# Sliding-window attention beside a long convolution on one core: three spectral products instead of four, folded filter blocks, and a common tile layout

## The chip, the cores and the metric

The kernel runs on one core of a Trainium2 chip. The metric is the device time of one execution in microseconds; "before" is the median of three runs. A profile shows one execution with a span from its first to its last instruction.

The engines are named as in the profile: PE (TensorE, matmuls; PEld is its loading of weights), DVE (VectorE), ACT (ScalarE), POOL (GpSimd), SP (SyncE, which here only issues DMAs). SPq, ACTq and POOLq are the queues from which DMAs are issued. Each engine works through its own queue in order and waits on semaphores of the others.

## The reference

Two independent computations over 2048 positions and 576 channels, joined along the channels:

```python
# a: attention, 32 heads of 18, each position sees itself and 7 earlier ones, two apart
q, k, v = split(x @ wqkv)                       # 2048x576 times 576x1728
logits[s, w] = q[s] . k[s - 2 w] * 18 ** -0.5   # w = 0..7, masked before position 0
o = sum_w softmax(logits)[s, w] * v[s - 2 w]
a = o @ wo
# b: short convolution, gate, long causal convolution per channel, gate
k_shift[s] = sum_t k[s - t] * shift_k[:, t]     # 4 taps
kv = k_shift * v
y = causal_convolution(kv, ssm_k, length 2048)  # written with an FFT of 4096
b = q * (y + kv * ssm_D)
out = concatenate([a, b], axis=-1)
```

## The kernel before

**Stages.** Everything lies in one instruction stream per engine, written out by Python code. In order of time: a head (constants, loading and turning x, tables of sines); the taps of the short convolution on DVE while PE projects q and k; the attention (logits, softmax, weighing of v) on DVE while PE projects v and makes spectra; the spectral products on DVE while PE sums them, turns them back and multiplies by wo; and a short tail.

**The long convolution.** The sequence is cut into four blocks of 512 (`NBL`, `BL`), and so is the filter. Each block gets a spectrum of length 1024 by matmuls with tables of sines and cosines. `filter_spectrum(m)` (L520) makes eight units per filter block: a frequency group `gi` of 128 by a cosine or sine part `cs`; each unit is four steps `c` of 128 positions, each of two matmuls in `mm3` (L515 and L516, 384 and 192 columns), and one eviction by ACT to `Ks` (L530). `turn_filter` then adds the neighbouring block's parts with accumulating DMAs on POOL's queue (L542). `x_spectrum(i)` (L579) does the same for a block of kv, with eight units of eight half-height matmuls (L586) evicted to `xw` (L589). The input block is folded about its middle first by `mirror` (L490).

The output block j is the sum over i of spectrum x[i] times filter[j - i]. `products(j, t, i)` (L856) makes all four products of the two real parts for one third t of the channels, 4 x 768 = 3072 columns, in one DVE instruction (L860); there are 30, over four buffers. `sums` (L867) adds them on PE with signed identity matrices, 16 matmuls for each (L880), and ACT evicts to `Yall` (L893). `inverse` (L900) transforms back, turns back by `flip` matrices and gates with q.

**Attention.** `logits` (L615) multiplies q by four shifted k's on DVE (4096 columns, L624) into two buffers, and PE sums over each head by the 0/1 matrices `E` (L633). `softmax` (L642) runs on DVE apart from the exponent on ACT (L658). `spread` (L694) copies the weights of one head group to all its channels by four DMAs on SP's queue (L701), for six chunks (two halves of positions by three channel groups). `weigh` (L713) multiplies them by v on DVE (L723, 18 instructions) and sums on PE (L739, L753). `output` (L776) multiplies by wo.

**What sets the order.** DVE's sequence is fixed by the program. PE's is woven: projections, spectra, mirrors, inverse and wo steps are units in the list `units`, and `until()` (L282) inserts the next few, as many as the next number in `PLACES` says, ahead of the PE work of the current DVE step. `need(label)` inserts all up to a label. PSUM offers two double banks under each of the tags A and B, so a unit also waits until ACT has evicted the one two before it under its tag.

**Places of the change.** v's weights are loaded by `load_w` into a corner of `Ks` and copied into head order by `reorder` (five ACT copies, L561) among the first filter units. Tables come from `table_k(0..3)` and `table_x(0..1)` (two tensor_scalars at L373 and one at L374 on DVE, one sine at L375 on ACT for each). The D term is added through the matrix `ones0` and the row `Drow`. Spread weights lie in the tile `X0`, in `qk` and in `pv`.

## Time and profile before

| What | Value |
|---|---|
| runs | 224.41, 224.32, 224.28 us; median 224.32 |
| profiled execution | 225.0 us, of which the span is 223.0 |
| granted PE clock | 1.00 |
| ACT busy | 154.4 us |
| taps on DVE | 16.8 to 61.0 us |
| logits, softmax and weighing on DVE | 61.2 to 160.4 us |
| spectral products on DVE | 160.4 to 215 us |
| last instructions of DVE | 218.66 us |
| `attn` spreads on SP's queue | first issue at 99.23, last issued by 142.9 us |
| filter transposes on SP's queue | issued 40.4 to 48.7 and 50.5 to 59.4 us, 5.0 to 10.5 us to landing |

The page lists for each group of instructions the line, engine and operation, the tiles written and read, the shapes, the count, the busy time in us with the mean of one in ns, and then how long the engine was idle just before them and what ended that. In the timeline the columns are start, duration, engine, line, operation, and in brackets the idle time before. In the list of waits they are the waiter, whom it waited for, the total in us, how often, and the longest.

### The profile page before, as it was taken

To read this page: it belongs to the slowest core of one execution; us is meant where nothing else is said; L and a number is where in the kernel's file an instruction comes from. 1 tells how busy PE (TensorE), PEld (TensorE's weight loads), DVE (VectorE), ACT (ScalarE), POOL (GpSimd) and SP (SyncE) were. 2 spreads that over 40 slices of the span, in tenths; PEclk is the share of its full clock that TensorE was granted. 3 is DMA by queue.
4 is the path that set the end of the run, shared out by engine and by line. 5 is a ranking of instruction groups with operands and counts; after the bars stand their busy time and mean duration, and the time that the engine had idled before them with its cause. 6 is when DMAs were issued, how large, how long until landed. Compare 5 with 4: busy or idle time off the path is not lost.

```text
span 223.0 us, 5309 instructions
## 1 busy us (share of the span) xinstructions
PE 213.1 (96%) x2271; PEld 118.2 (53%) x2271; DVE 208.1 (93%) x156; ACT 154.4 (69%) x213; POOL 31.9 (14%) x68
## 2 busy tenths in 40 slices
PE   7999999999999999999999999999999999999891
PEld 2543444444566556753444445665656667666560
DVE  7789999999988999999899999999999899999992
ACT  5858766888596987756667768885678887655630
POOL 8860000000000040403410000015000000330000
PEclk9999999999999999999999999999999999999999
DMA  5999999999900047659999469917211103662016
GB/s 187 274 229 219 188 241 203 221 207 235 216 0 0 3 83 131 117 95 169 198 190 235 124 114 203 225 32 234 88 56 53 57 3 107 199 208 75 3 53 159
DMA packets 30985, 31.41 MB, mean 141 GB/s; under 512 B 16849, under 2 KB 26705, under 8 KB 30962
## 3 DMA queue, kind: packets, MB, share of 16 engines
q1 hardware_dynamic: 25714, 21.93, 44.6%
q0 software_dynamic: 2624, 6.64, 14.6%
q10 hardware_dynamic: 2624, 2.51, 3.3%
q8 instruction: 17, 0.28, 0.5%
q14 instruction: 6, 0.05, 0.1%
HBM read 13.11 MB, written 4.72 MB: 80 GB/s over the span
## 4 chain that ended last, share of the span: by engine, by line
PE 76%; DVE 9%; ACT 5%; issue 4%; DMA 3%; SPq 1%; DVEq 0%; ACTq 0%
PE ps_proj L310 15%; PE ps_fk L515 10%; PE ps_wo L792 7%; PE ps_fx L586 6%; DVE qk L860 6%; PE ps_z L880 5%; PE ps_log L633 5%; PE ps_fk L516 5%; PE ps_acc L739 4%; PE ps_inv L912 4%; PE ps_proj L427 3%; PE ps_proj L315 3%; DMA X<-attn 3%; PE ps_proj L322 3%; PE ps_idle L138 2%
## 5 line engine op out<-in xcount | busy, mean ns | idle before, releaser
L860 DVE TENSOR_TENSOR qk<-xw,Ks 128x3072 bf16<-128x3072 bf16 x30 | 50.5, 1750 | 1.2 <-PE ps_z L880 1.0
L624 DVE TENSOR_TENSOR prod<-qk 128x4096 bf16<-128x4096 bf16 (+1 forms) x20 | 40.6, 2074 | 3.4 <-PE ps_log L633 3.3
L310 PE MATMUL ps_proj<-xw 128*128 128x512 bf16 x160 | 38.4, 380 | 0.0
L515 PE MATMUL ps_fk<-kTok,TK 128*128 128x384 bf16 x128 | 32.8, 327 | 0.6 <-ACT Ks L530 0.5
L516 PE MATMUL ps_fk<-kTok,TK 128*128 128x192 bf16 x128 | 31.4, 246 | 0.0
L530 ACT ACTIVATE Ks<-ps_fk 128x576 bf16<-128x576 f32 x32 | 20.4, 653 | 9.9 <-PE ps_fk L516 9.7
L310 PEld LDWEIGHTS <-xw 128*128 128x128 bf16 x160 | 14.3, 98 | 18.9 <-issue 4.9
L893 ACT ACTIVATE Yall<-ps_z 128x768 bf16<-128x768 f32 x23 | 17.4, 808 | 6.1 <-PE ps_z L880 5.9
L346 ACT ACTIVATE qk<-ps_proj 128x1024 bf16<-128x1024 f32 x14 | 14.4, 1027 | 7.1 <-PE ps_proj L310 3.4
L589 ACT ACTIVATE xw<-ps_fx 128x576 bf16<-128x576 f32 x32 | 18.6, 660 | 0.2
L515 PEld LDWEIGHTS <-TK 128*128 128x128 bf16 x128 | 12.5, 98 | 11.8 <-issue 4.2
L792 PE MATMUL ps_wo<-qk,pv 128*128 128x288 bf16 x128 | 17.9, 287 | 0.0
L586 PE MATMUL ps_fx<-ab,TX 64*128 64x288 bf16 x256 | 17.7, 283 | 0.0
L487 DVE TENSOR_TENSOR ab<-ab,tB 128x2304 bf16<-128x2304 bf16 x12 | 16.3, 1358 | 0.4
L880 PE MATMUL ps_z<-qk,ident 64*64 64x384 bf16 x288 | 16.4, 325 | 0.3 <-ACT pv L743 0.3
L484 DVE TENSOR_TENSOR tB<-kj,skb 128x2304 bf16<-128x2304 bf16 x12 | 16.3, 1356 | 0.3
L912 PE MATMUL ps_inv<-Yall,TI 128*128 128x288 bf16 (+1 forms) x112 | 15.5, 292 | 0.7 <-ACT Yall L893 0.6
L739 PE MATMUL ps_acc<-P,ident 64*64 64x512 bf16 x192 | 15.3, 379 | 0.0
L346 ACT ACTIVATE v<-ps_proj 128x1024 bf16<-128x1024 f32 x9 | 9.2, 1022 | 8.8 <-PE ps_proj L322 4.6
L586 PEld LDWEIGHTS <-TX 64*128 64x128 bf16 x256 | 11.7, 94 | 6.5 <-issue 3.6
L799 ACT ACTIVATE qk<-ps_wo 128x576 bf16<-128x576 f32 x16 | 10.4, 651 | 6.1 <-PE ps_wo L792 3.0
L792 PEld LDWEIGHTS <-pv 128*128 128x128 bf16 x128 | 11.5, 98 | 6.0 <-issue 3.2
(146 smaller groups left out, 352.8 us busy)
## 6 DMA issues: line engine op xcount, KB each, us to landing
kj<-in_B_k_dram SPq DMA_DIRECT2D x7, 504.0 KB, 8.1
Ks<-Ks POOLq DMA_DIRECT2D x6, 576.0 KB, 7.7
qk<-attn SPq DMA_DIRECT2D x12, 256.0 KB, 5.8
vt<-in_B_v_dram SPq DMA_DIRECT2D x8, 288.0 KB, 8.6
out_dram<-qk ACTq DMA_DIRECT2D x8, 288.0 KB, 2.9
X<-attn SPq DMA_DIRECT2D x8, 256.0 KB, 5.1
Ks<-in_A_x_dram SPq DMA_DIRECT2D x2, 576.0 KB, 5.2
xw<-in_A_wqkv_dram SPq DMA_DIRECT2D x2, 576.0 KB, 7.4
```

Source lines behind the costliest of these rows:

```text
L310: nc.tensor.matmul(ps[:, jp, :], wq(kb, comp, 128 * ct, 128), xT(kb, 1024 * jj + 512 * jp, 512), start=(kb == 0 and not first), stop=(kb = ...
L346: nc.scalar.activation(view(t, o + pad + 1024 * jj, [[512, 2], [1, 512]]), ps[:], ACT.Copy)
L515: nc.tensor.matmul(o[:, 0:2], w, rhs[:, 0:2], start=start, stop=stop)
L516: nc.tensor.matmul(o[:, 2], w, rhs[:, 2], start=start, stop=stop)
L530: nc.scalar.activation(view(Ks, (3 - m) * SPB + 4 * D * cs + 96 * gi, [[768, 3], [384, 2], [1, 96]]), acc3(ps), ACT.Copy, scale=(CSG, SSG) ...
L586: nc.tensor.matmul(ps[:, pm, 0:HD], TX[64 * pm:64 * pm + 64, c, 128 * gi:128 * gi + 128], kv[64 * pm:64 * pm + 64, c, HD * h:HD * h + HD], ...
L624: r = dve(1024 * nj, lambda: nc.vector.tensor_tensor(view(prod, 0, [[256 * nj, 4], [256, nj], [1, 256]]), view(t, o + 256 * hh, [[0, 4], [ ...
L739: nc.tensor.matmul(acc[64 * o:64 * o + 64, h, :], ident[64 * h:64 * h + 64, 64 * h:64 * h + 64], view(P, 256 * u, [[2048, 2], [1, 256]])[6 ...
L792: nc.tensor.matmul(ps[:, r, 0:HD], oT(hh, j + 2 * r, t)[:, o:o + 128], wo[:, t // 2, t % 2, HD * h:HD * h + HD], start=(t == 0 and h == 0) ...
L860: r = dve(3072, lambda: nc.vector.tensor_tensor(pr, view(xw, i * SPB + 4 * TH * t, [[4 * D, 2], [0, 2], [1, 4 * TH]]), view(Ks, (3 - j + i ...
L880: nc.tensor.matmul(view(acc[r], 512 * h, [[192, 2], [96, 2], [1, 96]])[o:o + 64], w[64 * h:64 * h + 64, 64 * h:64 * h + 64], pr[64 * h:64 ...
L912: nc.tensor.matmul(ps[:, c, 0:n], TI[:, sl, pm, 128 * c:128 * c + 128], Yall[:, j % 2, pm, sl, c0:c0 + n], start=(pm == 0 and sl == 0), st ...
```

## The change

- **Products.** The spectra are held as sum and difference of their parts ("turned basis"), and each block of `xw` and of `Ks` has three parts: two from the evictions, and a third, their sum, that DVE adds when a block is first used (six additions of 768 and six of 2304 columns). A product is then 3 x 768 = 2304 columns; three buffers instead of four. PE's sums use identities of 1 and 2 with signs; their number stays at 480.
- **Filter blocks.** `fold_filter` folds a block about its middle: per block 8 or 12 matmuls (`ps_rev`), two ACT evictions of 576 columns scaled by 0.5, a scaling of one row on POOL, and an accumulating DMA of 2 x 576 columns for the partner. A spectrum unit then has two steps instead of four (for two of eight units one more, with the constant `two`). `table_k` runs twice instead of four times. D is added to the filter's first row by a DMA; `first_rows` exchanges rows by six DMAs of one row on SP's queue.
- **v's weights** are loaded once and read by PE with a step of nine elements, 64 columns at a time (`wa`), instead of being copied in order by ACT.
- **Softmax.** The reciprocal of the sums on DVE becomes Ln and Exp(-x) on ACT.
- **Layout.** `xw`, `Ks`, `TB`, `av`, `v` and `qk` are cut into equal parts of 2304 columns (`HB`), and kv, the tables, the spread weights and the products lie in parts that are free at that time.
- **Order.** `PLACES` has new numbers; `FKS` and `FXS` weave v's projection and x's spectra into the filter's units; the narrow channel group of each half is weighed first; wo's first half starts earlier; the first logits are preceded by an `until()`.

POOL gets eleven further small instructions that make constants (`flip1`, `flip0`, `corner`, `two`, `ident2` and others) behind the old ones, and five memsets in the table.

```diff
-    XW = 2 * SPB
-    xw = main.tile([128, 4 * SPB], BF16, name="xw")
-    TK = main.tile([128, 4, 2, BL], BF16, name="TK", tag="tabk")
-    TX = main.tile([128, 4, BL], BF16, name="TX", tag="tabx")
+    xw = main.tile([128, 12 * HB], BF16, name="xw")
+    XO = 8 * BL
+    TB = main.tile([128, XO + 4 * BL], BF16, name="TB")
+    TK = view(TB, 0, [[2 * BL, 2], [BL, 2], [1, BL]])
+    TX = view(TB, XO, [[BL, 4], [1, BL]])
     TI = main.tile([128, 4, 2, 256], BF16, name="TI")
+    XG = (9, 0, 3, 6)
+    KVS = (0, 2, 1, 8)
+    def kv_of(i):
+        return view(xw, HB * KVS[i], [[D, 4], [1, D]])
     def xT(kb, t0, n):
-        return view(xw, XW + SPB * (t0 // 1024) + 1024 * kb + t0 % 1024, [[1, n]])
+        return view(xw, HB * (3 + 3 * (t0 // 1024)) + 1024 * kb + t0 % 1024, [[1, n]])
     def x5(jj):
-        return view(xw, XW + SPB * jj + 4096, [[1, 512]])
+        return view(xw, HB * (3 + 3 * jj) + 4096, [[1, 512]])
+    def w_at(kb, comp):
+        return HB * (9, 10, 5)[comp] + D * kb if kb < 4 else 11 * HB + D * (1, 2, 0)[comp]
     def wq(kb, comp, c0, n):
-        return view(xw, comp * 5 * D + kb * D + c0, [[1, n]])
-    wv = view(xw, 0, [[5 * D, 3], [D, 5], [1, D]])
+        return view(xw, w_at(kb, comp) + c0, [[1, n]])
+    def wa(kb, a):
+        return view(xw, w_at(kb, 2) + a, [[9, 64]])
...
+    def k_at(m, part):
+        return 3 * HB * (3 - m) + HB * part
+    def kTok(m):
+        return view(Ks, k_at(m, 2), [[D, 4], [1, D]])
...
+            for kb in range(4):
+                se = dict(start=(kb == 0 and not first), stop=(kb == 3 and first))
+                if ct < 4 and comp < 2:
+                    nc.tensor.matmul(ps[:, jp, :], wq(kb, comp, 128 * ct, 128), xT(kb, 1024 * jj + 512 * jp, 512), **se)
+                    continue
+                for e in range(2):
+                    w = wa(kb, min(2 * ct + e, 8)) if comp == 2 else wq(kb, comp, 512, 64)
+                    nc.tensor.matmul(ps[64 * e:64 * e + 64, jp, :], w, xT(kb, 1024 * (jj if ct < 4 else e) + 512 * jp, 512),
+                                     tile_position=(0, 64 * e), **se)
...
-        return table(n_all[:, 2 * c:2 * c + 2, :], TK[:, c, :, :], n_all[:, 8, :], (c, c), 2048, (512.0, 0.0))
+        return table(n_all[:, 2 * c:2 * c + 2, :], TK[:, c, :, :], n_all[:, 8, :], (2 + c, 2 + c), 2048, (256.0, 1792.0))
...
-    sines = [table_k(2), table_k(3), table_x(0), table_x(1)]
-    sines[0]()
+    sines = [table_x(0), table_x(1)]
...
+    def first_rows():
+        nc.gpsimd.dma_start(row(0, 0), B_ssm_D.unsqueeze(0), accum_op=ALU.add)
+        spare = [view(Ks, k_at(1, 0) + D * m, [[1, D]])[0:1] for m in range(2)]
+        for step in range(3):
+            for m in (1, 0):
+                nc.sync.dma_start(*((spare[m], row(m, 0)), (row(m, 0), row(m, 1)), (row(m, 1), spare[m]))[step])
+    def fold_filter(m):
+        kt, swapped = kTok(m), m < 2
+        nc.gpsimd.tensor_scalar(row(m, 2), row(m, 2), 0.5 ** 0.5, None, op0=ALU.mult)
+        def unit():
+            pss = [bank2("ps_rev", "A") for _ in range(2)]
+            for c in range(2):
+                turns = [(flip1 if swapped else flip0, 1 - c), ((identn0, identn)[c], 2 + c)]
+                if not swapped:
+                    turns.insert(1, (corner, c))
+                for n, (w, of) in enumerate(turns):
+                    for h in range(2):
+                        nc.tensor.matmul(pss[c][:, h, 0:HD], w[:], kt[:, of, HD * h:HD * h + HD], start=(n == 0),
+                                         stop=(n == len(turns) - 1))
+            for c in range(2):
+                nc.scalar.activation(halves(kt[:, c, :]), pss[c][:, :, 0:HD], ACT.Copy, scale=0.5)
+                pe(0.5, "A", 0.65)
+            nc.gpsimd.dma_start(view(Ks, k_at(m, 2) + 2 * D, [[1, 2 * D]]), view(Ks, k_at(m, 2), [[1, 2 * D]]),
+                                accum_op=ALU.add, max_dma_last_dim=2 * D)
+        return (1.0, unit, f"fold{m}")
     def filter_spectrum(m):
         def unit(gi, cs):
             tag = filler_tag("fk", "AAB") if logits_run[0] else "A"
             ps = bank2("ps_fk", tag)
-            skip = m == 0 and cs == 0
-            for c in range(4):
-                mm3(ps, TK[:, c, cs, 128 * gi:128 * gi + 128], thirds(kTok[:, m, c, :]), c == 0, c == 3 and not skip)
-            if skip:
-                mm3(ps, ones0[:], thirds(Drow[:]), False, True)
-            nc.scalar.activation(view(Ks, (3 - m) * SPB + 4 * D * cs + 96 * gi, [[768, 3], [384, 2], [1, 96]]), acc3(ps), ACT.Copy,
-                                 scale=(CSG, SSG)[cs][m] * 2.0 / 1024.0)
-            pe(1.0, tag, 0.65)
-            if (gi, cs) == (3, 1) and m < NBL - 1:
+            extra = cs == 0 and gi in (1, 2)
+            for c in range(2):
+                mm3(ps, TK[:, c, cs, 128 * gi:128 * gi + 128], thirds(kTok(m)[:, 2 * (1 - cs) + c, :]), c == 0,
+                    c == 1 and not extra)
+            if extra:
+                mm3(ps, two[:], thirds(kTok(m)[:, 0, :]), False, True)
+            nc.scalar.activation(view(Ks, k_at(m, cs ^ (m & 1)) + 96 * gi, [[768, 3], [384, 2], [1, 96]]), acc3(ps),
+                                 ACT.Copy, scale=(PSG, MSG)[cs][m] * 2.0 ** 1.5 / 1024.0)
+            pe(0.5, tag, 0.65)
+            if (gi, cs) == (3, 0) and 0 < m < NBL - 1:
                 turn_filter(m + 1)
-        for gi in range(4):
-            for cs in range(2):
-                units.append((1.0, partial(unit, gi, cs), "fk"))
+        for cs in (1, 0):
+            for gi in range(4):
+                units.append((0.5, partial(unit, gi, cs), f"fk{m}"))
+    def half(t, at):
+        return view(t, at, [[1, HB]])
+    def add_half(t, to, of):
+        nc.gpsimd.dma_start(half(t, to), half(t, of), accum_op=ALU.add, max_dma_last_dim=HB)
     def turn_filter(m):
-        for cs in range(2):
-            nc.gpsimd.dma_start(Ks[:, 3 - m, cs], Ks[:, 4 - m, 1 - cs], accum_op=ALU.add, max_dma_last_dim=2304)
-    for m in reversed(range(NBL)):
-        filter_spectrum(m)
+        for part in range(2):
+            add_half(Ks, k_at(m, part), k_at(m - 1, part))
...
-            wraw = view(Ks, 3 * SPB, [[D, 5], [1, D]])
-            load_w(nc.sync, 2, wraw)
+            load_w(nc.sync, 2)
             for m in range(1, NBL):
                 load_filter(m)
-            def reorder(kb):
...
-                units.insert(6 + 3 * kb, (0.0, partial(reorder, kb), "wv"))
...
+            nc.scalar.preload_act_table_set("natural_log_exp_and_others")
...
+    vs = deque(made(project, 2, 2) + made(project, 2, 0) + made(project, 2, 1))
+    fxs = deque(u for i in (0, 2, 1, 3) for u in made(x_spectrum, i))
+    rest = []
+    for n, count in enumerate(FXS):
+        for _ in range(min(count, len(fxs) - (24 if n < 5 else 8))):
+            rest.append(fxs.popleft())
+        rest += [vs.popleft(), vs.popleft()]
+    rest = deque(rest + list(fxs))
+    first_rows()
+    fks = []
+    for m in reversed(range(NBL)):
+        fks += made(filter_spectrum, m)
+        if m > 1:
+            fks.insert(len(fks) - 4, fold_filter(m - 2))
+    for count, u in zip(FKS, fks):
+        for _ in range(min(count, len(rest))):
+            units.append(rest.popleft())
+        units.append(u)
+    units.extend(rest)
...
-        with nc.allow_low_precision(reason="the weights are bf16"):
-            dve(256, lambda: nc.vector.reciprocal(part, total), ns=6.5)
-        r = dve(2048, lambda: tt(at, at, part.unsqueeze(1).to_broadcast([128, W, 256]), ALU.mult))
+        r = clk["D"]
+        nc.scalar.activation(total, total, ACT.Ln)
+        nc.scalar.activation(part, total, ACT.Exp, scale=-1.0)
+        clk["A"] = max(clk["A"], r) + 0.75
+        r = dve(2048, lambda: tt(at, at, part.unsqueeze(1).to_broadcast([128, W, 256]), ALU.mult), clk["A"])
...
-    chunks = [(hh, c) for hh in range(2) for c in range(3)]
...
+    chunks = [(hh, c) for hh in range(2) for c in (2, 0, 1)]
...
-        X = (X0[:], qk[:, 0:4096], pv[:, 4608:8704], X0[:], qk[:, 4096:8192], qk[:, 0:4096])[n]
-        Xt[n] = X
+        t, at, step = ((TB, 0, 2048), (Ks, k_at(3, 2), 3 * HB), (qk, 4608, 2048), (TB, 0, 2048),
+                       (Ks, k_at(3, 2), 3 * HB), (TB, 0, 2048))[n]
+        Xt[n] = view(t, at, [[step, 2], [256, W], [1, 256]])
...
-        pr = view(qk, 3072 * (npr[0] % 4), [[1536, 2], [768, 2], [1, 768]])
+        pr = view(*((av, 0), (v, 6912), (qk, 9216))[npr[0] % 3], [[QTR, 3], [1, QTR]])
         npr[0] += 1
-        r = dve(3072, lambda: nc.vector.tensor_tensor(
-            pr, view(xw, i * SPB + 4 * TH * t, [[4 * D, 2], [0, 2], [1, 4 * TH]]),
-            view(Ks, (3 - j + i) * SPB + 4 * TH * t, [[0, 2], [4 * D, 2], [1, 4 * TH]]), ALU.mult))
+        r = dve(3 * QTR, lambda: nc.vector.tensor_tensor(
+            pr, view(xw, HB * XG[i] + QTR * t, [[HB, 3], [1, QTR]]),
+            view(Ks, k_at(j - i, 0) + QTR * t, [[HB, 3], [1, QTR]]), ALU.mult))
...
-        sc, ss = CSG[j - i], SSG[j - i]
-        for r, terms in enumerate((((0, 0, sc), (1, 1, ss)), ((1, 0, sc), (0, 1, -ss)))):
+        m = j - i
+        for r in range(2):
+            sign = ((1, 1), (-1, 1), (-1, -1), (1, -1))[m][r]
+            terms = ((2, ident if sign > 0 else identn), (1 - r ^ (m & 1), identn2 if sign > 0 else ident2))
...
+            for new, tile_, at in ((last == 0, Ks, k_at(j, 0)), (last == j, xw, HB * XG[j])):
+                if new and (j == 0 or t == 0):
+                    at, w = (at + QTR * t, QTR) if j == 0 else (at, HB)
+                    a, b, c = (view(tile_, at + HB * part, [[1, w]]) for part in range(3))
+                    dve(w, lambda: nc.vector.tensor_tensor(c, a, b, ALU.add))
```

199 lines of the change are left out of this document (105 added, 94 removed).

## The prediction

> **What bounds the kernel now.** I read the busy shares first, then VectorE's timeline, then the waits and the chain of waits. The busy line names two candidates:
>
> ```profile
> PE 213.1 (96%) x2271; PEld 118.2 (53%) x2271; DVE 208.1 (93%) x156; ACT 154.4 (69%) x213; POOL 31.9 (14%) x68
> ```
>
> PE's share is of pipelined spans, so I trust DVE's more: 208.1 of 223.0 us leave 14.9 us idle. DVE's timeline at the places that decide:
>
> ```profile
> 16.47 0.42 DVE L404 COPY xw<-ps_x 128x512 bf16<-128x512 bf16 x1 [0.94 <-PE ps_x L402]
> 16.82 1.35 DVE L484 TENSOR_TENSOR ab<-kj,skb 128x2304 bf16<-128x2304 bf16 x1
> 18.08 1.35 DVE L484 TENSOR_TENSOR tB<-kj,skb 128x2304 bf16<-128x2304 bf16 x1
> ...
> 61.16 4.49 DVE L624 TENSOR_TENSOR prod<-qk 128x4096 bf16<-128x4096 bf16 x2
> ...
> 95.70 1.75 DVE L665 RECIPROCAL attn<-attn 128x256 bf16<-128x256 f32 x1
> 97.49 1.23 DVE L666 TENSOR_TENSOR attn<-attn,attn 128x2048 bf16<-128x2048 bf16 x1
> ...
> 160.41 15.29 DVE L860 TENSOR_TENSOR qk<-xw,Ks 128x3072 bf16<-128x3072 bf16 x9
> ```
>
> From 16.8 us on DVE hardly rests: taps to 61, attention to 160, spectral products to 216, then a tail. Its waits behind the head are few:
>
> ```profile
> DVE prod L624 <- PE ps_log L633: 3.3, 6, 1.1
> DVE qk L860 <- PE ps_z L880: 1.0, 1, 1.0
> DVE ab L484 <- DMA kj<-in_B_k_dram: 0.5, 1, 0.5
> ```
>
> The logits stage (61 to 113) is where DVE waits for PE: products wait until PE has summed an older one, and PE has filter units between. So the gain of a change is what it takes from DVE's queue after 16.8 us, plus at most the 3.3 us of logits waits. The groups that carry prices:
>
> ```profile
> L860 DVE TENSOR_TENSOR qk<-xw,Ks 128x3072 bf16<-128x3072 bf16 x30 | 50.5, 1750 | 1.2 <-PE ps_z L880 1.0
> L530 ACT ACTIVATE Ks<-ps_fk 128x576 bf16<-128x576 f32 x32 | 20.4, 653 | 9.9 <-PE ps_fk L516 9.7
> L561 ACT ACTIVATE xw<-Ks 128x576 bf16<-128x576 bf16 x5 | 6.4, 1285 | 0.0
> L315 PEld LDWEIGHTS <-xw 128*64 128x64 bf16 x48 | 2.6, 109 | 2.8 <-issue 1.3
> ```
>
> **Spectral products.** Thirty products shrink from 3072 to 2304 elements. Old ones start 1.68 us apart (50.5 / 30). Independent 2304-element ones start 1.27 us apart (16.82 to 18.08 above): 30 x 0.41 = -12.3 us. The basis needs third parts, twelve additions on DVE: six of 768 at 0.55 (the 768-element gate at L921 takes 546 ns; overlapping, 3.2 in all) and six of 2304, whose product waits for them, at the 1.40 of the dependent taps (19.46 to 20.86): 8.4. Net **-0.7 us**: the three multiplications are nearly paid for in additions. PE's sums stay at 480 matmuls. Products rotate over three buffers instead of four, so product n+3 waits for PE's sums n: three products of 1.27 cover 3.8 us, where 5.0 were covered; in the new order at most 24 inverse matmuls (0.12 each) and 16 of turning back (0.05) stand between two sums, 3.7 us. I leave the wait of 1.04 as it is; bounds -1.0 and +2.0.
>
> **Tables.** Four tensor_scalars of 494 ns and two of 694 leave DVE before 16.5 us, two sines (1.15) leave ACT. Worth 3.4 us on DVE, but the row at 16.47 waits for PE's turned x: that end stays, and the taps start at 16.8 as before. **0**; bounds -0.5 and 0.
>
> **Filter spectra.** In the chain one pair (384 and 192 columns) takes 0.245 us of PE. 132 pairs (32.3 us) become 72 (17.6); the fold adds 40 matmuls of 288 columns at 0.122 (four mirrors take 0.49): 4.9. PE gives back 9.8 us between 57 and 100. But each unit is still evicted by ACT at 0.65, with PE now needing 0.5 instead of 0.98: the unit's pace falls from 0.98 to 0.65, a third. So I let a third of the logits waits go: **-1.1 us**; bounds -3.3 (all) and +1.0 (eight fold evictions of 0.65 stand ahead of the first logits; the six x units pulled ahead add 3.9 of ACT there). The fold's partner is made by an accumulating DMA on POOL's queue (the old 576 KB ones land after 7.7 us, these are half): the first is issued near 60 and its user stands four units, two v units and three logits behind, near 75, so it is covered; if not, PE loses up to 7.7. The first two folds stand ahead of the last mirrors on PE and wait for two filter transposes, issued from 40.4 and 50.5 and 5 to 10.5 us to landing: by 61 at the latest, when the mirrors' taps end anyway. The filter's row copies (six 1 KB DMAs on SP in three dependent steps) and POOL's four scalings run from 60 on, 15 us before the second fold and 35 before the spreads behind them in SP's queue; POOL's eleven new instructions for constants (0.1 to 1.1 each) move the pads of k from 13.5 to near 20, wanted at 61.
>
> **Softmax denominators.** The reciprocal costs DVE 1.79 (95.70 to 97.49), twice. In its place ACT takes Ln and Exp of 256 elements, bounded by its 256-wide eviction (390 ns) and the 128x1 activation (203): about 0.8 plus hand-overs, 0.9. Nothing of DVE's stands between, so DVE waits, and everything in ACT's queue is ahead: at the first, five filter evictions behind the exponent (3.3 us against DVE's 1.64 of sums); at the second, an attention eviction, whose PE sum (1.85) starts with DVE's last product: 1.85 + 1.03 + 0.8 = 3.7 against 1.64 + 1.79 = 3.4. So -0.4 and +0.2: **-0.2 us**; bounds -1.8 and +2.0.
>
> **v in the new order.** The five copies L561 (6.4 us of ACT, off the path) go; v's weights are read with a step of nine elements, 64 columns at a time: 128 matmuls in 64 pairs instead of 64 full ones, and eight pairs that were narrow already. PE's streaming is the same, as L315 shows: eight such matmuls in 0.98 us, 0.245 a pair, their loads (109 ns) hidden. A stepped read has one price here: L561 reads every ninth element in 1285 ns where a plain 576 takes 653, 1.1 ns more for each. 64 columns: 109 + 70 = 180 ns, below the 216 of a pair: **0**, if a pair's two loads overlap each other as L315's do (48 x 109 = 5.2, busy 2.6). If not, 0.36 a pair: 72 x 0.14 = 10.1 us of PE.
> [...]
>
> **Attention transfers.** The narrow chunk goes first, so the second spread is wanted at DVE's second weighing product (117.9) instead of its fifth (129.1), the third at its sixth (131.4) instead of its ninth (138.2). L701's transfers land 5 to 10 us after issue from 99 on. I take 0; bounds 0 and +2.5.
>
> **The sum.** -0.7 - 1.1 - 0.2 = -2.0 us. The profiled execution took 225.0 (span 223.0 and 2.0 around): 223.0 by that. The median of the runs is 224.32, 0.7 lower, so the forecast is **222.3 us**, products starting near 159.
>
> **Rivals.** *The room is used in full* (A): PE's 9.8 us end all logits waits (-3.3), ACT answers at once (-1.8), the buffers never hold (-1.0), -0.7: -6.8, 217.5. For it: PE is the chain through all of 61 to 130. Against: the pace set by ACT. *Nothing left* (B): Ln and Exp wait their turn at both places (+2.0), and that takes the 1.8 of the rest: 224.5. For it: ACT's queue is in order and 0.69 full; against: the overlap above. *The stepped loads show* (C, slower): the loads of v's pairs come one after the other or slower. Up to 216 ns a pair it is free; from 216 + 9800 / 72 = 352 on it has eaten the filter's relief, and each further 10 ns costs 0.72. At 0.36 the stage is as long as now (no -1.1), and the 16 pairs between the two first attention sums put the second Ln 2.2 us later: 224.3 - 0.7 - 0.2 + 2.2 = 225.6; at 0.43, twice the pair's matmuls, 72 x 0.07 = 5 more, about 230. That the products do not become a quarter shorter (D): 12.3 us worse, 234.6; the 2304-element rows are this very form, so only a few in a hundred.
>
> **Chances.** Forecast 0.45 (its own range 220.5 to 223.8), A 0.22, B 0.11, C 0.20, D 0.02. The 80% range takes in A and the near half of C: **217 to 226.5**. A difference of 0.2%, 0.45 us, is about what can be told from none. Faster: forecast and A, 0.67; same: B, 0.11; slower: C and D, 0.22.
>
> **What would show it.** Products x30 near 1350 ns, twelve additions worth 11 to 12 us; first tap at 16.8, first logits product at 61; DVE's logits waits near 2 us; Ln and Exp near 0.4 each, and DVE's idle ahead of the last softmax multiply about 1.6 each; loads of v's weights at 180 ns or less with pairs 0.22 to 0.25 apart. Wrong it is if taps end well before 61, if the loads exceed 216 ns, if DVE waits for PE in the products by more than 2 us, or if a spread arrives late.

## The result, and the profile after

| | before | after |
|---|---|---|
| median of 19 runs each, taken side by side | 224.49 us (223.93 to 225.56) | 225.58 us (224.35 to 227.58) |
| ratio, with its 95% interval | | 1.0042 [1.0022, 1.0061] |
| profiled execution, and its span | 225.0 / 223.0 us | 224.35 / 222.6 us |

The changed kernel is slower by 1.1 us, while its profiled execution, the shortest of the 19, is shorter by 0.65. So one trace against one trace tells the wrong sign here, and what follows goes by several executions of each.

The busy line of the page after:

```profile
PE 208.3 (94%) x2271; PEld 120.7 (54%) x2271; DVE 201.3 (90%) x160; ACT 150.8 (68%) x218; POOL 47.0 (21%) x91
```

VectorE (DVE) lost 6.8 us of work and the span 0.4: DVE stands idle for 21.3 us instead of 14.9. Its timeline at the places shown of before:

```profile
16.35 1.35 DVE L523 TENSOR_TENSOR xw<-kj,skb 128x2304 bf16<-128x2304 bf16 x1
...
61.57 4.96 DVE L711 TENSOR_TENSOR av<-qk 128x4096 bf16<-128x4096 bf16 x2
67.54 4.49 DVE L711 TENSOR_TENSOR av<-qk 128x4096 bf16<-128x4096 bf16 x2 [1.02 <-PE ps_log L720]
...
97.50 1.23 DVE L755 TENSOR_TENSOR av<-av 128x2048 bf16<-128x2048 bf16 x1 [1.11 <-ACT av L753]
...
161.25 1.36 DVE L951 TENSOR_TENSOR av<-xw,Ks 128x2304 bf16<-128x2304 bf16 x1
```

The taps start 0.5 us earlier than before, and the first logits product 0.4 us later; its pair takes 4.96 us where it took 4.49. DVE's waits, and the groups with prices:

```profile
DVE av L711 <- PE ps_log L720: 3.1, 6, 1.0
DVE av L755 <- ACT xw L753: 2.3, 1, 2.3
DVE av L755 <- ACT av L753: 1.1, 1, 1.1
```

```profile
L951 DVE TENSOR_TENSOR av<-xw,Ks 128x2304 bf16<-128x2304 bf16 x10 | 13.5, 1354 | 0.5
L601 ACT ACTIVATE Ks<-ps_fk 128x576 bf16<-128x576 f32 x32 | 18.3, 660 | 1.8 <-PE ps_fk L555 1.7
L357 PEld LDWEIGHTS <-xw 128*64 128x64 bf16 x176 | 14.9, 178 | 5.5 <-issue 3.1
L571 POOL TENSOR_SCALAR Ks<-Ks 1x576 bf16<-1x576 bf16 x4 | 8.4, 2114 | 37.7 <-DMA Ks<-in_B_ssm_k_dram 37.7
```

The waits for logits sums are what they were (3.1 for 3.3) although the filter's spectrum matmuls are nearly halved. The wait of 1.0 in the products is gone, two waits for ScalarE (ACT) have come, and L571, which the prediction set at nothing, is 2.1 us for one row. The row of L951 is one of three buffers, ten products of the thirty; the 178 ns of L357 is the mean of two kinds of loads.

**Where the time went.** The table lays side by side the traces of three executions of the kernel before, two of the changed kernel at a granted clock of 0.997 and more, and two at 0.991. The numbers are means from the timelines in us, and the single values agree within 0.6. The eleventh logits product is the first one of the second half; the expectations below call it the tenth.

| From, to | before | after, full clock | difference | after, at 0.991 |
|---|---|---|---|---|
| second `B_k` transfer there, first logits product | 32.91 | 33.65 | +0.74 | 33.71 |
| to the eleventh logits product | 22.71 | 23.70 | +0.99 | 25.18 |
| to the first softmax multiply | 13.30 | 12.23 | -1.07 | 12.23 |
| to the first weighing product | 15.26 | 15.13 | -0.13 | 15.14 |
| to the last gate, behind the spectral products | 101.59 | 100.44 | -1.15 | 100.52 |
| to DVE's last instruction pair | 4.32 | 5.28 | +0.96 | 5.28 |
| to the end of the span | 4.37 | 4.44 | +0.07 | 4.72 |
| sum | 194.46 | 194.87 | +0.4 | 196.8 |

The transfer itself comes at 27.9 to 28.6 us in both. So the change gains 2.35 us in three stages and loses 2.76 in the other four. The two executions at 0.991 lose 1.5 more between the first and the eleventh logits product, and some 0.4 in all behind it. Executions at 0.992 or less of the full clock are 12 of 31 of the changed kernel (median span 224.75, the other 19: 223.5), against 2 of 101 of the kernel before (median span of all: 222.8). Where the clock fell in the ten that were not traced is not shown.

### The profile page after: what moved, and what is told of

It reads as the page before. It is cut to its first block, busy times and chain, and to the rows that moved or that the text cites. A ratio compares the mean times of both kernels' runs of the same rounds, so it can differ in the third digit from the quotient of the medians.

```text
span 222.6 us, 5352 instructions
## 1 busy us (share of the span) xinstructions
PE 208.3 (94%) x2271; PEld 120.7 (54%) x2271; DVE 201.3 (90%) x160; ACT 150.8 (68%) x218; POOL 47.0 (21%) x91
## 3 DMA queue, kind: packets, MB, share of 16 engines
HBM read 13.11 MB, written 4.72 MB: 80 GB/s over the span
## 4 chain that ended last, share of the span: by engine, by line
PE 55%; DVE 15%; ACT 13%; DMA 7%; SPq 5%; issue 3%; DVEq 0%
PE ps_z L972 9%; PE ps_proj L357 8%; PE ps_wo L881 7%; PE ps_acc L828 7%; PE ps_inv L1004 7%; DVE tB L523 6%; DVE xw L526 6%; ACT Ks L601 5%; PE ps_fx L658 5%; DMA kj<-in_B_k_dram 4%; PE ps_log L720 4%; DMA Ks<-in_A_x_dram 3%; SPq L214 3%; ACT xw L661 2%; PE ps_fk L554 2%
## 5 line engine op out<-in xcount | busy, mean ns | idle before, releaser
L711 DVE TENSOR_TENSOR av<-qk 128x4096 bf16<-128x4096 bf16 (+1 forms) x20 | 41.1, 2098 | 3.3 <-PE ps_log L720 3.1
L353 PE MATMUL ps_proj<-xw 128*128 128x512 bf16 x96 | 22.9, 380 | 0.0
L985 ACT ACTIVATE av<-ps_z 128x768 bf16<-128x768 f32 x23 | 17.4, 809 | 7.0 <-PE ps_z L972 7.0
L357 PE MATMUL ps_proj<-xw 128*64 128x512 bf16 x176 | 21.8, 391 | 0.0
L881 PE MATMUL ps_wo<-qk 128*128 128x288 bf16 x128 | 18.5, 287 | 0.4 <-ACT qk L832 0.4
L658 PE MATMUL ps_fx<-xw,TB 64*128 64x288 bf16 x256 | 17.2, 283 | 1.0 <-ACT Ks L601 0.8
L357 PEld LDWEIGHTS <-xw 128*64 128x64 bf16 x176 | 14.9, 178 | 5.5 <-issue 3.1
L554 PE MATMUL ps_fk<-Ks,TB 128*128 128x384 bf16 x64 | 17.2, 327 | 0.1
L1004 PE MATMUL ps_inv<-av,TI 128*128 128x288 bf16 (+1 forms) x112 | 16.1, 292 | 0.7 <-ACT av L985 0.6
L526 DVE TENSOR_TENSOR xw<-xw,tB 128x2304 bf16<-128x2304 bf16 x12 | 16.3, 1358 | 0.4
L571 POOL TENSOR_SCALAR Ks<-Ks 1x576 bf16<-1x576 bf16 x4 | 8.4, 2114 | 37.7 <-DMA Ks<-in_B_ssm_k_dram 37.7
L555 PE MATMUL ps_fk<-Ks,TB 128*128 128x192 bf16 x64 | 15.7, 246 | 0.0
```

What stands on the lines that cost most here:

```text
L353: nc.tensor.matmul(ps[:, jp, :], wq(kb, comp, 128 * ct, 128), xT(kb, 1024 * jj + 512 * jp, 512), **se)
L357: nc.tensor.matmul(ps[64 * e:64 * e + 64, jp, :], w, xT(kb, 1024 * (jj if ct < 4 else e) + 512 * jp, 512), tile_position=(0, 64 * e), **se)
L526: dve(2304, lambda: nc.vector.tensor_tensor(kv, kv, o, ALU.add))
L658: nc.tensor.matmul(ps[:, pm, 0:HD], TX[64 * pm:64 * pm + 64, c, 128 * gi:128 * gi + 128], kv[64 * pm:64 * pm + 64, c, HD * h:HD * h + HD], ...
L711: r = dve(1024 * nj, lambda: nc.vector.tensor_tensor(view(prod, 0, [[256 * nj, 4], [256, nj], [1, 256]]), view(t, o + 256 * hh, [[0, 4], [ ...
L881: nc.tensor.matmul(ps[:, r, 0:HD], oT(hh, j + 2 * r, t)[:, o:o + 128], wo[:, t // 2, t % 2, HD * h:HD * h + HD], start=(t == 0 and h == 0) ...
```

## The experiments

**More executions.** Both kernels again, unchanged, with intervals, and later one trace more of the kernel before and two of the changed one.

> The kernel before, unchanged, so that its executions can be laid beside those of the changed kernel. Theory 1 (the changed kernel's median is longer than its profiled execution because TensorE, which has less to do in it, gets a lower granted clock in most of its executions): the kernel before shows a granted clock of 0.998 or more in nearly all executions and spans within 1 us of 223.0. Rival (executions of both kernels spread alike, and the profiled one of the changed kernel was merely a lucky one against a steadier cause of 1 us): clocks of the kernel before go down to 0.992 as well, with spans of 224 and more.

> The changed kernel, unchanged. Theory 1: spans of 222.6 to 225.7 us again, the longer ones at a granted clock of 0.992 to 0.997, the short ones at 0.999 to 1.000; where the profile falls on a long one, the clock is below full in one stretch, and the milestones after this stretch are late by what the span is longer. Rival: clock and span go independently of one another, and the late milestones are spread over the whole kernel. Ratio to the kernel before 1.002 to 1.006 under both.

> The changed kernel once more, for one more traced execution. Counted from the arrival of the second B_k transfer (27.86 us in the first trace, 28.14 in the second) the rest of the span is 194.7 to 195.0 us at full clock. If executions without a fall of the clock are longer than those of the kernel before for a reason of the change, this rest is what differs (kernel before: 194.25 and 194.75); if it is the arrival of the transfer, it stays and the arrival is later.

> The same again. Should this execution be one with the clock at 0.992 or less, the fall lies between 62 and 68 us, the third logits product starts 1.5 us or more later against the first than the 5.97 us of the other traces, and everything behind it by as much.

> The kernel before once more, for the same two numbers: arrival of the second B_k transfer (28.25 and 28.55 so far) and the rest of the span (194.75 and 194.25).

Measured: before 224.85 us (its clock goes down to 0.993 too, with spans of 222.8 to 223.1 there; in the traced one of these it falls in the last slice of the span). Against the executions taken beside it this same kernel comes to 1.0023 [0.9996, 1.0050], and three of its twelve spans are 223.7 to 224.4 at a clock of 0.997 and more: so 0.5 us can come without any change. After: 226.06, again 1.0042 [1.0008, 1.0075], six of twelve executions at 0.990 to 0.992, with spans of 223.8 to 225.1. The two traces hit two such executions, 226.93 and 227.06 us. The rest of the span is 194.8 and 195.0 at full clock, 196.3 and 197.2 in these. TensorE's (PE's) timeline where they differ, first of the first trace, then of the second execution at 0.991:

```profile
60.39 0.41 PE L581 MATMUL ps_rev<-Ks,identn 128*128 128x288 bf16 x2
61.49 0.65 PE L535 MATMUL ps_fold<-xw,fold 128*128 128x288 bf16 x4 [0.69 <-DVE xw L527]
62.63 0.95 PE L535 MATMUL ps_fold<-xw,fold 128*128 128x288 bf16 x4 [0.49 <-ACT xw L536]
63.77 3.12 PE L658 MATMUL ps_fx<-xw,TB 64*128 64x288 bf16 x48 [0.20 <-ACT xw L536]
66.82 1.05 PE L720 MATMUL ps_log<-av,E 128*32 128x512 bf16 x16
```

```profile
61.80 0.65 PE L535 MATMUL ps_fold<-xw,fold 128*128 128x288 bf16 x4 [1.34 <-DVE xw L527]
62.94 0.94 PE L535 MATMUL ps_fold<-xw,fold 128*128 128x288 bf16 x4 [0.49 <-ACT xw L536]
64.08 4.79 PE L658 MATMUL ps_fx<-xw,TB 64*128 64x288 bf16 x48 [0.20 <-ACT xw L536]
68.80 1.05 PE L720 MATMUL ps_log<-av,E 128*32 128x512 bf16 x16
```

PE stands idle ahead of the last fold and in it, and then the same 48 matmuls take 4.79 us instead of 3.12; the first logits sums start that much later. The work by stretches (the first columns: stretch, its length, PE busy; the clock stands behind POOL), of the kernel before, the first trace after, and the second execution at 0.991:

```profile
57.00:64.00 7.00, 6.45 (x53) 4.46 (x50) 6.80 (x5) 4.71 (x8) 0.18 (x2) 1.00 0.64 143
64.00:68.00 4.00, 4.00 (x43) 2.44 (x41) 2.95 (x2) 2.72 (x5) 0.00 (x0) 1.00 0.00 0
```

```profile
57.00:64.00 7.00, 4.79 (x35) 3.05 (x35) 6.80 (x5) 5.26 (x9) 4.72 (x7) 1.00 0.85 170
64.00:68.00 4.00, 4.00 (x66) 2.88 (x62) 2.98 (x2) 3.63 (x7) 4.00 (x3) 1.00 0.62 89
```

```profile
57.00:64.00 7.00, 4.21 (x28) 2.55 (x27) 6.76 (x5) 4.59 (x9) 5.39 (x7) 1.00 0.91 177
64.00:68.00 4.00, 3.92 (x38) 3.04 (x39) 2.83 (x2) 2.60 (x6) 4.00 (x2) 0.57 0.52 76
```

PE is idle for 0.55 of the 7 us before, for 2.2 after, for 2.8 in the execution whose clock then falls to 0.57 on the mean of the next four us. This idle time is called the hole below.

**Is it the hole?** Two experiments on that: the hole made in the kernel before, and idle work put into the hole of the changed kernel.

```diff
-    16, 6, 8, 11, 1, 0, 5,     # e4_before_gap: kernel before, PLACES
+    16, 6, 8, 8, 4, 0, 5,
```

> The kernel before with three of its filter units (24 matmuls, 2.9 us of TensorE) moved from ahead of the last fold to just behind it; nothing else. It gives the kernel before the hole that the changed kernel has between 57 and 64 us. Theory 1 (a hole there makes the granted clock fall in a share of the executions): a third or more of them at 0.992 or less, where the kernel before has few. Theory 2 (TensorE is the bound from 64 on, so a hole before it is paid back in full): the wait before the third logits product grows from 1.05 to 2.5 to 4 us, and the spans at full clock lengthen by 1.5 to 2.9 us. Rivals: the clock stays as in the kernel before, and then the fall belongs to something else in the changed kernel (its stepped weights, its DMAs); or the wait stays near 1 us, and then VectorE bounds that stage.

```diff
+        if i == 3:              # e2_warm: ahead of each half of the last mirror
+            ps = bank2("ps_idle", "A")
+            for _ in range((3, 2)[n]):
+                nc.tensor.matmul(ps[:, 0, :], ident[:], view(TB, XO, [[1, 512]]), start=True, stop=True)
```

> The changed kernel with five idle matmuls (128x512, 216 ns each, into a free PSUM buffer) before the two halves of the last fold (three and two), where TensorE stands idle for 0.69 to 1.46 us and 0.49 us; nothing else differs. Theory 1 (in the slower executions the granted clock falls to a half for 3 us from 64 on, as seen in the changed kernel with the reciprocal, because TensorE is emptier from 57 to 64 than before): the clock stays at 0.995 and more, no execution has a span over 224.3, the median falls by 0.6 to 1.2 us to 224.4 to 225.2. Rival (the clock falls for another reason, or its fall costs nothing): executions at 0.990 to 0.992 stay and the median stays within 0.3 us of 225.8.

The kernel before with the hole, here 3.33 us of the 7 in which PE is idle, takes 230.31 us, 1.025 [1.0228, 1.0272]. All four executions are at 0.982 to 0.992, with spans of 228.0 to 228.4. Its stretches and DVE's third product:

```profile
57.00:64.00 7.00, 3.67 (x21) 2.31 (x20) 6.76 (x6) 2.86 (x4) 0.18 (x2) 0.73 0.70 154
64.00:68.00 4.00, 4.00 (x22) 2.52 (x21) 2.09 (x1) 2.14 (x4) 0.00 (x0) 0.63 0.00 0
```

```profile
71.85 10.09 DVE L624 TENSOR_TENSOR prod<-qk 128x4096 bf16<-128x4096 bf16 x5 [5.76 <-PE ps_log L633]
```

So a hole there makes the clock fall in either kernel: none of the change's weights or transfers is needed for it. The wait of 5.76 is larger than the 2.5 to 4 expected: the hole is paid back, and the granted clock is 0.52 on the mean from 60 to 64 and 0.63 from 64 to 68. How much each of the two costs isn't separated, since none of the four executions was at full clock and the two at 0.992 have the spans of the two at 0.982 and 0.983. With five idle matmuls the changed kernel's PE is idle for 1.1 of the 7 us, none of twelve executions is under 0.994, and the median is 225.45, 1.0022 [0.9999, 1.0044]. By the ratios this is 0.45 us better than the changed kernel, not 0.6 to 1.2, the two intervals overlap, and one span was 224.6. So the count of the falls is what this run shows, and its time alone wouldn't show what they cost. An estimate from the traces: the falls cost 12/31 x 1.5 = 0.6 us on the mean, and the other 0.4 is the change's own. The mean spans split it about evenly: 222.9 for the kernel before, 223.4 for the 19 executions without a fall, 223.9 for all 31.

**The row scalings on ACT.** L571 issued on ACT instead of POOL.

```diff
-        nc.gpsimd.tensor_scalar(row(m, 2), row(m, 2), 0.5 ** 0.5, None, op0=ALU.mult)
+        nc.scalar.activation(row(m, 2), row(m, 2), ACT.Copy, scale=0.5 ** 0.5)
```

> The changed kernel with the four scalings of one row each (L571, GpSimd, 2114 ns each) issued on ScalarE instead. Theory (VectorE's instruction that runs beside one of them takes 0.35 to 0.47 us longer, 1.3 us in all before the first logits product): the taps at 50.9 and 57.0 and the first logits product take 1.36, 1.36 and 4.49 us again, the first logits product starts 0.8 us earlier, and the time falls by 0.5 to 1.3 us. Rival (ScalarE's work on the filter spectra, 18.9 of 20 us in the stretch from 80 to 100, is what is late there): the taps shorten but the softmax starts when it did, and the time stays within 0.3 us of the changed kernel.

DVE's taps in the changed kernel and POOL's rows beside them:

```profile
50.92 1.82 DVE L523 TENSOR_TENSOR tB<-kj,skb 128x2304 bf16<-128x2304 bf16 x1
52.77 1.36 DVE L526 TENSOR_TENSOR xw<-xw,tB 128x2304 bf16<-128x2304 bf16 x1
...
56.95 1.70 DVE L523 TENSOR_TENSOR tB<-kj,skb 128x2304 bf16<-128x2304 bf16 x1
```

```profile
50.48 2.02 POOL L571 TENSOR_SCALAR Ks<-Ks 1x576 bf16<-1x576 bf16 x1 [33.71 <-DMA Ks<-in_B_ssm_k_dram]
56.45 1.97 POOL L571 TENSOR_SCALAR Ks<-Ks 1x576 bf16<-1x576 bf16 x1 [3.94 <-DMA Ks<-in_B_ssm_k_dram]
```

With the scalings on ACT all taps take 1.35 or 1.36, the first product starts at 60.75 instead of 61.57 (the transfer came within 0.01 us of the same time) and its pair takes 4.50. So it is the scalings on POOL that slow DVE's instructions, as expected to the number. But the time didn't fall: the median is 226.18, 1.0068 [1.0044, 1.0092]. The next row shows why:

```profile
69.04 2.29 DVE L711 TENSOR_TENSOR av<-qk 128x4096 bf16<-128x4096 bf16 x1 [3.79 <-PE ps_log L720]
```

The third product waits for 3.79 us instead of 1.02, since PE's filter fold waits 1.81 for the scaling in ACT's queue. The third product hangs on PE, and this edit puts a new wait into PE's queue. So it shows what slows the taps, but not what shorter taps would be worth without that wait.

**The reciprocal back on DVE.**

```diff
-        nc.scalar.activation(total, total, ACT.Ln)
-        nc.scalar.activation(part, total, ACT.Exp, scale=-1.0)
+            nc.vector.reciprocal(part, total)
```

> The changed kernel with VectorE's reciprocal in place of Ln and Exp on ScalarE in both softmax stages. By the prediction's sum: 0.2 us longer (0.4 in the first softmax, less 0.2 given back in the second). Rival (what ScalarE is spared counts, since it is the late one at both places: Ln and Exp there begin only after an eviction of 1.02 us): the second softmax multiply starts up to 0.5 us earlier against the end of the sums, the first no later than now, and the time falls by 0.2 to 0.6 us.

From the end of the sums to the multiply: 1.82 and 1.82 us, where the changed kernel has 1.11 and 2.29. So Ln and Exp gain 0.71 in the first softmax and lose 0.47 in the second, 0.24 in all, as in the sum. Not all of it arrives: from the first multiply to the first weighing product the kernel with the reciprocal needs 14.81 us instead of 15.13, so counted from the eleventh logits product its second multiply is not later but 0.1 earlier. The median, 227.03 or 1.0087 [1.0052, 1.0122], is longer by more than any of this, with five of eight executions at 0.991 or less. The edit lies behind the place where the clock falls, so this kernel is read by its trace, and the rest of its time stays open.

**Other places for the work around the hole.** Six kernels, all meant to shorten the third product's wait.

```diff
-    6, 0, 0, 2, 2, 0,            # e2_order: FKS, the x units behind three filter units
+    0, 0, 0, 2, 2, 6,
-    18, 6, 7, 10, 3, 3, 0, 5,    # e3_place: PLACES, three x units behind the first sum
+    18, 6, 7, 10, 3, 0, 3, 5,
-    18, 6, 7, 10, 3, 3, 0, 5, 0, 3, 0, 4, 5, 1, 0, 10, 0, 2, 3, 5, 2,    # e4_fewer: PLACES
+    18, 6, 7, 10, 3, 3, 0, 3, 0, 2, 0, 4, 4, 1, 0, 10, 0, 2, 3, 9, 2,
```

> The changed kernel with the order of the work on TensorE after the taps altered: the six units of the input's transform (L658), which wait for the last taps' fold and ScalarE's eviction of it, no longer stand ahead of the first logits sums (L720) and the filter's half-length units (L554), but behind the first three of these. Theory (the wait of 1.02 us before the third logits product and the late softmax come from this new chain of fold, eviction and input transform, not from the length of the filter units): the wait before the third product falls under 0.4 us, the tenth product starts 0.6 to 1.0 us earlier and the span falls by as much in executions at full clock; TensorE also has other work there, so the clock falls less often. Rival (ScalarE's 18.9 of 20 us from 80 to 100 decides): the third product starts earlier, the last softmax multiply of the first half does not.

> The order of the run before, and besides the four row scalings (L571, GpSimd) on ScalarE at places where it waits: two before the last projection's eviction at 56.8, one each some units ahead of the two later filter folds. Theory (two causes that add up, the slowed taps and the chain behind them): taps and first products at 1.36 and 4.49 us again, the first logits product 0.8 us earlier than in the changed kernel as it was with the scalings moved alone, and now the wait before the third product does not give it back: the span falls by 1.2 to 2.0 us against the changed kernel, to 221 to 221.8, and the time lies under the kernel before. Rival: the gain ends at the same ScalarE-bound place near 97 us and the two together bring no more than the order alone.

> The changed kernel with one place moved: three of the six input transform units that stand ahead of the first logits sum on TensorE go behind it; nothing is moved past a fold this time (in the order tried before, the fold of a later filter block came up early and waited 1 to 3 us for its row exchange). Theory (the wait of 1.02 us before the third product is the first sum queued behind six units that themselves wait for the last fold): that wait falls to 0.1 us or less, and everything behind it starts about 0.9 us earlier, with a span near 222 at the same arrival of the B_k transfer. Rival (another wait takes it up: the later ones of 0.30, 0.56, 0.41 and 0.62 us grow, since TensorE and ScalarE are as full): the tenth product starts less than 0.4 us earlier counted from the first product.

> The same place moved, and the four row scalings on ScalarE at places where it waits. Counted from the arrival of the second B_k transfer (27.86 us in the changed kernel's profile) the first logits product comes at 32.9 instead of 33.7 us, the first two products take 4.49 instead of 4.96 us. Theory (the two causes add): 1.6 to 2.2 us less than the changed kernel in executions at full clock. Against it: TensorE's gap before the last fold; if theory 1 holds the granted clock falls in as many executions as in the changed kernel.

> The run before with two idle matmuls (128x512) ahead of each half of the last fold. Theory 1: no execution under 0.994 granted clock, and a median up to 0.7 us below that of the run before; with the two causes above 222.8 to 224.0 us, under the kernel before. Rival: the idle matmuls delay the fold by up to 0.4 us and the clock is as in the run before, so that the median is the same or longer.

> The changed kernel with four units of other work (value projection, filter) taken out from between the logits sums of the third, fifth and eighth product and put behind the first softmax. Theory (TensorE stays full from 64 to 97 because other units took the room of the shortened filter units, so the waits for the logits sums, 3.1 us, are those units' queue): the four waits up to the eighth product fall by 1.0 us or more in all, the tenth product starts 1 us earlier; what is gained comes back behind the first softmax, where the four units (2 us) now stand in front of the logits sums, and the span changes by less than 0.7 us either way. Rival (there is room for them there): the span falls by about the same 1 us.

All are slower than before: 1.0100, 1.0190, 1.0059, 1.0064, 1.0084 and 1.0298 (the intervals reach 0.002 to 0.004 either way). In the first two a later filter fold came up early and waited 1.1 and 2.9 us on PE for its row exchange. The cleanest is the fourth, whose waits for logits sums are:

```profile
61.70 4.50 DVE L716 TENSOR_TENSOR av<-qk 128x4096 bf16<-128x4096 bf16 x2
66.54 4.49 DVE L716 TENSOR_TENSOR av<-qk 128x4096 bf16<-128x4096 bf16 x2 [0.34 <-PE ps_log L725]
73.02 3.43 DVE L716 TENSOR_TENSOR av<-qk 128x2048 bf16<-128x2048 bf16 x2 [1.99 <-PE ps_log L725]
```

The wait of 1.02 has become 0.34, and the next, 0.30 in the changed kernel, is 1.99: the rival of the third kernel, word for word. PE's queue from the last fold to the fifth product's sums is what it was, and only its order changed. Here the taps are short too, and the first product comes 32.9 us behind the transfer instead of 33.65; yet the eleventh comes at 57.6, where the changed kernel's two traces have 57.3 and 57.4. The scalings on ACT again hold up PE's filter folds, for 0.88 and 0.68 us instead of 0.28 and 0.42. The third kernel was at 0.992 or less in eight of eleven executions, the fourth in three of seven. The fifth, with two and two idle matmuls, had two of six at 0.988 or less, against the expectation: PE is still idle for 2.15 of the 7 us in its trace, which holds no fall. The sixth shortened two waits by 0.6 us together, and three later ones came or grew, to 1.22, 1.23 and 2.28: its traced span is 5 us longer than the changed kernel's, not 0.7.

**The hole filled with the filter's own units.** Filter block 3 folded two units earlier and three of its units ahead of the last mirror; in the second kernel also three x units fewer ahead of the first sums.

```diff
+        if i == 3:
+            units.insert(3, fold_filter(3))
         until()
...
-            units.extendleft([fold_filter(m) for m in (3, 2)][::-1] + rest)
+            units.extendleft(([fk3[0], fk3[1], fold_filter(2), fk3[2]])[::-1] + rest)
```

> The changed kernel with the hole filled with its own work: the fold of filter block 3, whose row comes at 50.5, goes ahead of the last two projections, and three of that block's filter units ahead of the last input fold (before, all of them stand behind it). If the hole is the one cause (it is paid back as waits for logits sums, and the granted clock falls in it), TensorE's idle time from 57 to 64 falls from 2.2 to under 1.2 us, executions at 0.992 or less get rare (under one in six), and the span at full clock falls by 0.5 to 1.5 us against the changed kernel, to 221.5 to 222.5. Rival: ScalarE, which must now evict these units as well between 57 and 64, delays the last fold, and the wait before the third product grows over 1.0 us; then the time stays.

> The same, and three fewer units ahead of the first logits sums (one instead of three before the first product, two instead of three before the first sum), since three have been done already. If TensorE's queue there sets the third product: wait before it 0.3 us or less and a span 0.3 to 0.8 us below the run before. Rival, as when three units were moved behind the first sum: the wait comes back at the fifth product.

Measured: 235.92 (1.0472 [1.0426, 1.0518]) and 227.30 us (1.0073 [1.0045, 1.0102], without two of its eight executions, which took 230.4 and 231.0 at 0.992 and 0.991). PE's idle time from 57 to 64 fell to 1.58 and 1.39 us, not under 1.2, and two of six and two of eight executions were still at 0.992 or less. The rival came true: in the first the last fold starts 1.17 us behind the first logits product instead of 0.08 ahead of it, and the third product waits 3.04 us, in the second 1.81. Each filter fold needs both PSUM buffers of its tag, and each buffer waits for ACT, so PE's idle time goes from one place to the next (0.52, 0.62, 0.25, 0.79 us). Why the first kernel loses as much as 9 us behind that was not followed up. No kernel tried beats the kernel before.

## Why the prediction was wrong

The forecast was 222.3 us, 2.0 less than the median of 224.32; the kernel came out 1.1 us slower than the one before it. By the steps of the prediction:

- **Products, -0.7.** Their own sizes were nearly right: products of 1.35 us 1.27 apart, additions that take 12.0 us of the stage (11.6 forecast). The wait of 1.04, which the sum left standing, went, so the stage gained 1.24; without that it would have gained 0.2. What was not in the sum is its end. DVE's last gate and its cast of the last sums, before, then PE's and DVE's timelines after:

```profile
214.33 1.35 DVE L966 TENSOR_TENSOR qB<-yA,qB 128x2304 bf16<-128x2304 bf16 x1
215.60 0.95 DVE L891 CAST Yall<-ps_z 128x768 bf16<-128x768 f32 x1
```

```profile
212.14 1.47 PE L1004 MATMUL ps_inv<-av,TI 128*128 128x384 bf16 x8
213.54 0.36 PE L972 MATMUL ps_z<-v,identn 64*64 64x384 bf16 x4
```

```profile
212.88 1.35 DVE L1058 TENSOR_TENSOR TB<-v,TB 128x2304 bf16<-128x2304 bf16 x1
215.09 0.96 DVE L983 CAST av<-ps_z 128x768 bf16<-128x768 f32 x1 [0.85 <-PE ps_z L972]
```

  The last gate starts 1.45 us earlier, but PE is still at an inverse transform, so the cast follows the gate's start by 2.21 us instead of 1.27. Of 1.24, 0.96 is given back: with products a quarter shorter, the last stretch is PE's.
- **Tables, 0.** The taps start 0.47 us earlier, but DVE still waits for the second `B_k` transfer (0.54 us), which comes no earlier in the one kernel than in the other: right.
- **Filter spectra, -1.1, with bounds of -3.3 and +1.0: the step that failed.** "PE gives back 9.8 us between 57 and 100", and a third of the logits waits were to go. The room was of the size forecast: by their share of PE's busy time the filter's matmuls, folds included, fell from 33.7 to 24.5 us. But it didn't reach the waits, which are 3.1 us for 3.3 where 2.2 were forecast. From 64 to 92 PE is full, as before: between 57 and 100 value projections take 4.7 us instead of 1.1, and x units 3.1 instead of none. Most of the rest, 1.7 us, lies where it can't be used: ahead of the last fold and in it, where PE waits for taps and evictions. The wait before the third product stays (1.05, 0.48 and 0.66 us in the three traces before, 1.02 after):

```profile
66.70 4.49 DVE L624 TENSOR_TENSOR prod<-qk 128x4096 bf16<-128x4096 bf16 x2 [1.05 <-PE ps_log L633]
```

  Up to the eleventh product the stage is 0.99 longer instead of 1.1 shorter; 0.47 of this is the slowed product of the next item, which leaves about +0.5 for this step, inside its bounds and with the other sign. And the hole brings what no term held: a granted clock of one half for 3.4 us in the two traces at 0.991. Executions at 0.992 or less are 12 of 31, which makes about 0.6 us on the mean by the estimate above.
- **"POOL's four scalings", set at nothing.** The first two begin when their rows land, at 50.5 and 56.5, not "from 60 on", the other two at 63.6, and DVE's instructions beside them are slowed: 0.81 us in the taps, seen as +0.74 before the first logits product, and 0.47 of the 0.99 after it. That the scalings do this is shown. What it costs at the end is open: PE's last fold waits for the taps (0.69 us in the first trace), so they are in the chain that holds the third product, and both ways of moving the scalings to ACT held up that chain in another place.
- **Softmax, -0.2.** -0.71 and +0.47 by the experiment: right where it was reckoned, though 0.32 of the 0.71 is given back before the weighing. Of the rest of the 1.07 in that stretch, 0.27 is a wait for the exponent that is gone.
- **v's weights, 0.** The 176 loads are 32 plain ones of 109 ns and 144 stepped ones of 188 to 217, 194 on the mean (the estimate was 180):

```profile
L357 PEld LDWEIGHTS <-xw x176: 106/191/217, 51.7 to 126.3; 128*64 128x64 bf16 x176
```

  The three numbers behind the colon are the shortest, the median and the longest in ns. Sixteen matmuls take 1.9 to 2.0 us where they took 1.92, so the term of 0 was right; only the first pair of a stretch, nine times in all, is followed after 0.32 us instead of 0.24. **Spreads, 0:** no weighing product waited for one by more than 0.3.
- **Rivals.** A had no room, as above. B, "nothing left", is the nearest by what happened, for another reason than Ln and Exp: without the falls the change is at +0.4. C's 225.6 is the measured 225.58 by luck: its cause, loads that show, is out.

Shown: the hole, that the clock falls in it or behind it, where the 0.4 us at full clock arise, and that eight other placements of the work don't gain. Open: what the scalings on POOL cost at the end, the exact split between the falls and the rest, and how much the executions between 0.993 and 0.997 owe to shorter falls (their spans have a median near 223.7, and no trace holds one with a fall at 64).

## What to carry to other kernels

Work taken from a busy engine counts only at the place where something waits for it: look at what stands ahead of the next wait in that engine's queue after the change, and whether the engine has anything to do there at all. A hole in TensorE's work can cost twice, once as work put off and once as a slower clock on the work behind it (in the kernel before with the hole a wait of 5.76 us instead of 1.05, and a granted clock of 0.63 from 64 to 68; the two are not separated), and one trace may not hold the second; so lay several executions side by side by milestones, with their granted clocks, before a change of half a per cent is explained. A small instruction on an engine set at nothing still has a start time: find what it waits for, and what runs beside it then.

## What was not expected of the hardware

- In the changed kernel the clock fell after PE had been thinly used, without one long gap: in the four traces of the changed kernel and its variants with a fall, PE was busy for 3.79 to 4.21 of the 7 us from 57 to 64, and its longest single gap was 1.9 us; with 4.32 and more none fell there in the traces of this stretch, and two at 4.08 and 4.10 had none. In the kernel before with the hole PE was busy for 3.67 of these 7 us; the granted clock was 1.00 from 57 to 60 and 0.52 on the mean from 60 to 64. In the changed kernel's traces the fall is to one half (0.50 from 65 to 67) and lasts 3.4 us (0.86 + 1 + 1 + 0.54 in the second execution, from the granted clocks of 0.57, 0.50, 0.50 and 0.73 in the four us from 64 to 68). Its executions at 0.992 or less are 12 of 31; why the others are not is not shown.
- A scaling of one row on GpSimd (1x576, 2.0 us) makes the VectorE instruction beside it 0.34 to 0.47 us longer (1.36 to 1.70 and 1.82, 2.28 to 2.75). What in the two engines makes it so is not shown.
- A weight load that steps over nine elements takes 194 ns on the mean for 64 columns, where a plain one took 109, and it costs next to nothing here: the matmul pairs stay 0.21 to 0.24 us apart, but for nine that are followed after 0.32.
